# Second input tile of the first quarter loaded in two halves and normalised in two pieces, with the written orders of that quarter replaced

## The chip, the cores and the metric

The kernel runs on one core of one Trainium2 chip. The metric is the device time of one execution in microseconds (us). The kernel before takes 618.46 us, the median of 3 runs that lie between 618.18 and 618.94 us.

## The reference

The input x has 2048 tokens of 640 numbers, all in float32. It is layernormed, goes through an attention and through a feed-forward block, and the product of the two is added to x:

```
xn  = layernorm(x)
qkv = xn @ wqkv                      # 32 heads of 20
for each token s: keys and values of the 8 tokens s, s-2, ..., s-14 (those below 0 masked)
o   = softmax(q . k * 20**-0.5) . v  # over the 8
s   = o @ wo
g   = silu(silu(xn @ w1) @ w2)       # w1 640 x 1536, w2 1536 x 640
out = x + s * g
```

## The kernel before, in words

The tokens are cut into four groups: two halves of the sequence times even and odd positions, since the attention steps by two. A group is four tiles of 128 tokens, numbered 0 to 3. A group's qkv product is made in four quarters of the heads, and a quarter in five chunks of 128 input features. Of each product in float32 three cheaper ones are made: an operand is split into a high part (a copy rounded to the format fp32r) and a low part (what is left), and high times high, low times high and high times low are summed in PSUM. So a weight chunk c of the first quarter goes through three steps: it is loaded by SyncE's DMA queue in two pieces (the q columns, L420, and the k and v columns, L421), its high part is made by ScalarE (`wh` c, L463), and its low part by GpSimd or VectorE (`wl` c, L466; `ON_DVE` lists those that VectorE makes).

The change lies in the first quarter of the first group (`first_quarter`), where nothing has been loaded yet. Tile t is loaded (`xin` t). VectorE takes its statistics over two halves of the row (`s` t `a` and `b`, L694) and joins them (`g` t, L696), ScalarE takes the root (`q` t, L506), VectorE the reciprocal (`r` t, L508) and then normalises the tile (`a` t j, L700). TensorE transposes the five chunks of the tile (`T` t, L729) into PSUM; ScalarE makes the high part of the transposed tile (`h` t j, L740) and VectorE the low part (`l` t j, L744). Tile 0 is treated apart: its transposed tile is also copied whole to SBUF (`f0` j, L707) and multiplied with the raw weights of chunks 0 to 2 in full float32 (`0f0` to `0f2`, two passes each, L756), since the split weights are not ready so early; its high and low parts for chunks 3 and 4 come from that copy (`h02` and `l02`, L714 and L716). All other products of the quarter are of L764. There are 51 of them. A product is written as tile, kind and chunk: `1h0` is tile 1's high part times the high part of weight chunk 0, `1x0` its low part times the high part, `1w0` its high part times the low part.

What sets the order: every operation is recorded with its engine, duration, reads and writes in `Weave`, a small planner. In the first quarter the order is written out by hand: `FIRST` is TensorE's, `ORDER` that of ScalarE, VectorE and GpSimd. The loads on SyncE's queue go by priority numbers: weight chunk k has 1 + k, and `X_AT` gives those of tiles 1 to 3. `EARLY` holds the landing times that the planner assumes for the first transfers. The planner runs when the program is built; on the chip each engine takes its instructions strictly in the order that came out, and waits on semaphores where an operand is not there. Eight semaphores serve SyncE's transfers in turn, so a transfer is issued only when the one eight places ahead has landed. After the first quarter the products of the second quarter follow (L824 to L826).

Of the kernel before, what the change touches and what calls it, by code (L numbers as in the profile page):

```python
# [14 lines left out]
P = 128  # L15
# [3 lines left out]
DC, FC = D // P, F // P  # L19
# [21 lines left out]
NB = P // B  # L41
SHIFT = 16
RUN = D
X_AT = 1.5, 3.5, 5.5
LOW_AT = 3
ON_DVE = (3, 6, 7, 8)
FIRST = """T00 T01 0f0 T02 0f1 T1 0f2 1w1 1h2 1h0 1h1 1x0 1x2 1h3 0h4 1w0 1w2 1x1 1x3 0x3 1h4 0h3 0w4
           0w3 1x4 T2 0x4 1w4 1w3 2w1 2h234 2h1 2w4 2x3 2x2 2x1 2x4 T3 2w23 2h0 2w0 3h2 3w0 3w1 3w4 3x4
           3x1 3x0 3h0 3h4 3h3 3w2 3x3 2x0 3x2 3h1 3w3"""
ORDER = {"ACT": """q0 f00 wh0 f01 q1 wh1 f02 h02 wh2 h10 h11 h12 wh3 wh4 q2 h20 q3 h21 h30 h31 wh5 h00""",  # L50
         "DVE": """wl1 s0a s0b g0 r0 wl2 a00 a01 a02 s1a s1b g1 r1 a10 s2a l10 s2b l11 l02 g2 l12 s3a
                   r2 wl3 a20 s3b g3 l20 l21 r3 a30 l30 l31 l00""",
         "POOL": """wl0 wl4"""}


# [16 lines left out]
class Weave:  # L72
# [8 lines left out]
    LANES = 8  # L81
    RATE = 310e3
    LAND = 1.9
    EARLY = 2.4, 2.9, 4.8, 5.6, 6.95, 8.15, 8.9, 9.9
    TABLE = 1.28
    PATIENCE = 1.8
    SOFT = 2.5
# [65 lines left out]
    def chain(self):  # L153

        for e, names in ORDER.items():
            row = [self.named[n] for n in names.split() if n in self.named and self.named[n].eng == e]
# [84 lines left out]
def local_attention_silu_ffn(ctx: ExitStack, tc: tile.TileContext, x, wqkv, wo, w1, w2, out):  # L241
    nc = tc.nc
# [8 lines left out]
    xg = x.rearrange("b (g p j) d -> (b g) p j d", p=P, j=J)  # L251
# [4 lines left out]
    def rows(view, g):  # L256
        h, par = groups[g]
        return view[h, :, par::2, :]
# [32 lines left out]
    XIN = sb.tile([P, T, D], F32, name="xin")  # L291
# [17 lines left out]
    def bank():  # L309
        i = take("acc", 6)  # L310
        return ACC[i], ("acc", i)
# [22 lines left out]
    def dma(fn, reads, writes, nbytes, prio, dur=0.45, late=0.0):  # L334
        add("SP", dur, fn, reads, writes, prio, nbytes=nbytes, late=late)
# [102 lines left out]
    def w_load():  # L438
# [24 lines left out]
        act(n, lambda: nc.scalar.activation(hi, raw, AF.Copy), kr, [kh], 1000 + due, name=f"wh{k}")  # L463
        pool_does = k < LO and k not in ON_DVE
        eng, cost, by = ("POOL", po(n), nc.gpsimd) if pool_does else ("DVE", dv(n), nc.vector)
# [25 lines left out]
    def load_x(g, t, n=1, prio=None):  # L491
        dma(lambda: nc.sync.dma_start(XIN[:, t:t + n], rows(xg, g)[:, t:t + n]), [],
            [("xin", u) for u in range(t, t + n)], n * P * D * 4, clock[0] if prio is None else prio,
            late=LATE if g else 0.0)
# [179 lines left out]
    def first_quarter(i):  # L674
# [8 lines left out]
        PARTS = ((0, 1), (1, 3), (3, DC)), ((0, 1), (1, 3), (3, DC)), ((0, 3), (3, DC)), ((0, 3), (3, DC))  # L683
        XF = O[:, 0, :]
        steps = FIRST.split()
        total = [sum(len(s) - 2 for s in steps if s[0] == str(t) and s[1] in "hxwf") for t in range(T)]

        def begin(t):

            st, ks = ST[t % 2], ("st", t % 2)  # L690
            for k in range(2):
                cs = slice(k * 320, (k + 1) * 320)
                kx = ("xin", t) if t or k else ("xin", t, "a")
                dve(320, lambda k=k, cs=cs: nc.vector.bn_stats(out=st[:, k, :], in_=XIN[:, t, cs]), [kx], [ks + (k,)], 1,  # L694
                    name=f"s{t}" + "ab"[k])
            dve(60, lambda: nc.vector.bn_aggr(out=MV[:, t, :], in_=st), [ks + (0,), ks + (1,)], [("mv", t)], 1, name=f"g{t}")  # L696
            ln_rstd(t, t + 1, 1, name=str(t))
            for j, (a, b) in enumerate(PARTS[0] if not t else ((0, DC),)):
                cs = slice(a * P, b * P)
                dve((b - a) * 80, lambda cs=cs: nc.vector.tensor_scalar(  # L700
                    out=XIN[:, t, cs], in0=XIN[:, t, cs], scalar1=MV[:, t, 0:1], scalar2=SD[:, 1, t:t + 1],
                    op0=OP.subtract, op1=OP.mult), [("rs", t), ("mv", t), ("xin", t)],
                    [("xn", t, k) for k in ((j,) if not t else range(len(PARTS[t])))], 1, lock=True, name=f"a{t}{j}")

        def full(j, a, b, tp, kp):

# [59 lines left out]
                more = 0.0  # L766

        given = {}
        for k in range(2):
            cs = slice(k * 320, (k + 1) * 320)  # L770
            dma(lambda cs=cs: nc.sync.dma_start(XIN[:, 0, cs], rows(xg, 0)[:, 0, cs]), [],
                [("xin", 0) if k else ("xin", 0, "a")], P * 320 * 4, -2)
        for k, p in enumerate(X_AT):
            load_x(0, k + 1, prio=p)
        for k in range(RING):
            w_load()
        whole = [early_raw[c] for c in range(DC)]
# [4 lines left out]
        for t in range(T):  # L782
            b, kp = bank()
            ps[t] = b, kp
        turned = [0]
        for step in steps:
# [7 lines left out]
            t, k, cs = int(step[0]), "hxwf".index(step[1]), step[2:]  # L794
# [110 lines left out]
    def wo_last(g, i):  # L905
# [23 lines left out]

        ORDER = steps(range(3)) + steps(range(3, DC))  # L930

        def whole(t, cols, a=0, b=15):
            for n in range(a, b):
                x, c, k = ORDER[n]
                tm_mm(banks, t, x[i][:, c, tsl(t)], ws[c][k], n == 0, n == 14, cols)
# [16 lines left out]
        def rest():  # L952
            for n, (x, c, k) in enumerate(ORDER):
                nc.tensor.matmul(lastb[:, :CB], x[i][:, c, tsl(t)], ws[c][k][:, CA:], start=n == 0, stop=n == 14)  # L954
# [115 lines left out]
```

## Time and profile before

| | |
|---|---|
| median of 3 runs | 618.46 us (618.18 to 618.94) |
| the profiled execution | 618.66 us |
| its span from first to last instruction | 616.9 us |
| TensorE busy in the span | 611.0 us (99%) |
| VectorE, ScalarE, GpSimd busy | 563.5, 310.4, 110.3 us |
| share of TensorE in the chain that ended last | 98% |

Times in the views are microseconds from the span's start. The profiled execution took 1.8 us more than its span, for what lies around it. The start of the first quarter is the stretch up to about 23.4 us, when the first product of the second quarter begins.

### The profile page before, as it was taken

The page shows a single profiled execution, that of the slowest core. Times are in us where ns is not written, and L with a number is a line of the kernel's source. Part 1 is how long each engine was busy: PE and PEld are TensorE (multiplying, and loading weights), DVE is VectorE, ACT ScalarE, POOL GpSimd, SP SyncE. Part 2 cuts the span into 40 slices and gives each one's busy share as a digit, 9 for nine tenths or more (in the row PEclk, how much of TensorE's full clock was granted, in tenths as well). Part 3 has the DMA queues.
Part 4 walks back from the last instruction along what each step waited for, and adds up shares of the span by engine and source line. Part 5 has one row for each costly group of instructions (what it writes and reads, how often), then busy time and mean ns, then how long its engine had stood idle before and what let it go on. Part 6 is the DMA issues. An engine that isn't in the chain of part 4 may idle for free.

```text
span 616.9 us, 9054 instructions
## 1 busy us (share of the span) xinstructions
PE 611.0 (99%) x3347; PEld 551.1 (89%) x3347; DVE 563.5 (91%) x584; ACT 310.4 (50%) x656; POOL 110.3 (18%) x167
## 2 busy tenths in 40 slices
PE   8999999999999999999999999999999999999997
PEld 6889999998889999999888999999888999999997
DVE  6578999999989998999999999999979999999964
ACT  5535658937376313851945512582496316152650
POOL 5500000011101133111212233111121213311100
PEclk9999999999999999999999999999999999999999
DMA  8999999867999998764799999955569999866642
GB/s 251 337 281 350 345 371 413 322 222 218 309 295 347 334 358 263 232 198 138 205 240 253 335 333 309 277 179 163 168 198 285 240 320 304 283 213 198 208 149 86
DMA packets 61513, 162.45 MB, mean 263 GB/s; under 512 B 6957, under 2 KB 25229, under 8 KB 61469
## 3 DMA queue, kind: packets, MB, share of 16 engines
q0 software_dynamic: 20016, 82.58, 44.4%
q1 hardware_dynamic: 41453, 79.29, 40.3%
q8 instruction: 26, 0.43, 0.3%
q14 instruction: 18, 0.15, 0.1%
HBM read 109.55 MB, written 34.16 MB: 233 GB/s over the span
## 4 chain that ended last, share of the span: by engine, by line
PE 98%; DMA 1%; DVE 0%; SPq 0%; issue 0%; ACT 0%
PE acc L853 22%; PE acc L856 15%; PE acc L824 10%; PE acc L825 10%; PE acc L826 10%; PE rot L973 9%; PE rot L974 9%; PE rot L972 9%; PE acc L764 2%; DMA xin<-in_A_x_dram 1%; PE rot L856 1%; PE rot L853 0%; PE acc L954 0%; PE rot L729 0%; DVE st L694 0%; PE acc L756 0%
## 5 line engine op out<-in xcount | busy, mean ns | idle before, releaser
L824 PE MATMUL acc<-w,thl 128*128 128x512 f32 (+1 forms) x300 | 112.5, 375 | 0.0
L826 PE MATMUL acc<-w,thl 128*128 128x512 f32 (+1 forms) x300 | 112.4, 375 | 0.0
L825 PE MATMUL acc<-w,thl 128*128 128x512 f32 (+1 forms) x300 | 112.4, 375 | 0.0
L853 PE MATMUL acc<-w,sh 128*128 128x384 f32 x384 | 111.5, 333 | 0.0
L856 PE MATMUL acc<-w,sh 128*128 128x256 f32 x384 | 107.1, 279 | 0.0
L978 ACT ACTIVATE sh<-rot 128x512 fp32r<-128x512 f32 x48 | 28.7, 598 | 146.1 <-PE rot L974 146.0
L974 PE MATMUL rot<-thl,w 128*128 128x512 f32 x240 | 93.6, 390 | 0.0
L973 PE MATMUL rot<-thl,w 128*128 128x512 f32 x240 | 93.6, 390 | 0.0
L972 PE MATMUL rot<-thl,w 128*128 128x512 f32 x240 | 93.5, 389 | 0.0
L662 DVE TENSOR_TENSOR pr<-e,kv 128x2560 f32<-128x2560 f32 x32 | 90.4, 2823 | 0.8
L627 DVE TENSOR_REDUCE l<-pr 128x128 f32<-128x2560 f32 x32 | 90.0, 2813 | 0.6
L624 DVE TENSOR_TENSOR pr<-q,kv 128x2560 f32<-128x2560 f32 x32 | 90.1, 2816 | 0.2
L667 DVE TENSOR_TENSOR pr<-pr 128x1280 f32<-128x1280 f32 x64 | 74.0, 1155 | 1.5
L856 PEld LDWEIGHTS acc<-w,sh 128*128 128x128 f32 x384 | 72.2, 188 | 0.9
L853 PEld LDWEIGHTS acc<-w,sh 128*128 128x128 f32 x384 | 72.1, 188 | 0.9
L451 POOL DMA_DIRECT2D w<-half_w x72 | 38.6, 536 | 190.0 <-PE rot L974 60.8
L451 POOL DMA_DIRECT2D w<-half_q x52 | 27.7, 533 | 242.1 <-PE rot L974 116.8
L824 PEld LDWEIGHTS acc<-w,thl 128*128 128x128 f32 x300 | 56.3, 188 | 8.9 <-ACT gate L1027 0.2
L826 PEld LDWEIGHTS acc<-w,thl 128*128 128x128 f32 x300 | 56.3, 188 | 8.6
L825 PEld LDWEIGHTS acc<-w,thl 128*128 128x128 f32 x300 | 56.3, 188 | 8.6
L853 PE MATMUL acc<-w,thl 128*128 128x384 f32 x225 | 63.1, 333 | 0.0
L540 ACT ACTIVATE xin<-sf 32x256 f32<-32x256 f32 (+1 forms) x144 | 54.6, 379 | 8.2 <-DVE sf L567 6.6
(100 smaller groups left out, 1040.0 us busy)
## 6 DMA issues: line engine op xcount, KB each, us to landing
w<-half_w POOLq DMA_DIRECT2D x72, 640.0 KB, 5.9
w<-half_q POOLq DMA_DIRECT2D x39, 512.0 KB, 4.6
half_w<-w SPq DMA_DIRECT2D x24, 640.0 KB
w<-half_wo POOLq DMA_DIRECT2D x15, 640.0 KB, 5.6
kv<-kv SPq DMA_DIRECT2D x15, 560.0 KB
half_q<-w SPq DMA_DIRECT2D x15, 512.0 KB
kv<-kv SPq DMA_DIRECT2D x15, 420.0 KB
w<-half_q POOLq DMA_DIRECT2D x13, 384.0 KB, 4.9
```

Source lines behind the costliest of these rows:

```text
L624: dve(2560, lambda t=t: nc.vector.tensor_tensor(out=PR, in0=win(qq[:, t:t + 2, :], W, 0), in1=win(kv[:, 0, t:t + 2, :], W, CQ), op=OP.mult ...
L627: dve(2560, lambda t=t: nc.vector.tensor_reduce(out=l[:, t:t + 2].rearrange("p t w h -> p (t w h)"), in_=PR.rearrange("p t w (h d) -> p (t ...
L662: dve(2560, lambda t=t, v=v: nc.vector.tensor_tensor(out=PR.rearrange("p t w (h d) -> p t (w h) d", d=DH), in0=e[:, t:t + 2].rearrange("p ...
L667: dve(2 * k * CQ, lambda k=k: nc.vector.tensor_tensor(out=PR[:, :, 0:k, :], in0=PR[:, :, 0:k, :], in1=PR[:, :, k:2 * k, :], op=OP.add), [] ...
L824: nc.tensor.matmul(o, hi, wh, start=c == 0, stop=False)
L825: nc.tensor.matmul(o, lo, wh, start=False, stop=False)
L826: nc.tensor.matmul(o, hi, wl, start=False, stop=c == DC - 1)
L853: nc.tensor.matmul(a[t][0][:, :CA], st, w[:, :CA], start=first, stop=last)
L856: nc.tensor.matmul(b[t // 2][0][:, h * CB:(h + 1) * CB], st, w[:, CA:], start=first and h == 0, stop=last, skip_group_check=True)
L972: nc.tensor.matmul(h, wh[:, cs], TH[i][:, c, :], start=c == 0, stop=False)
L973: nc.tensor.matmul(h, wh[:, cs], TL[i][:, c, :], start=False, stop=False)
L974: nc.tensor.matmul(h, wl[:, cs], TH[i][:, c, :], start=False, stop=c == DC - 1)
```

## The change

Tile 1 is loaded as tile 0 already was: two transfers of 320 columns each in place of one of 640. Its first statistics wait for the first half alone. It is normalised in two pieces, of chunks 0 to 2 and of chunks 3 and 4, and each piece has its own successors among the transposes. The priorities of tiles 2 and 3 on the load queue go from 3.5 and 5.5 to 5.5 and 7.5. The low parts of weight chunks 1 and 5 go from GpSimd to VectorE and that of chunk 7 from VectorE to GpSimd. `FIRST`, `ORDER` and `EARLY` have new contents.

```diff
-X_AT = 1.5, 3.5, 5.5
+X_AT = 1.5, 5.5, 7.5
-ON_DVE = (3, 6, 7, 8)
-FIRST = """T00 T01 0f0 T02 0f1 T1 0f2 1w1 1h2 1h0 1h1 1x0 1x2 1h3 0h4 1w0 1w2 1x1 1x3 0x3 1h4 0h3 0w4
+ON_DVE = (1, 3, 5, 6, 8)
+FIRST = """T00 T01 T02 0f0 0f1 T101 T12 0f2 1h0 1w1 1x2 1h2 1w2 1h1 1x0 0h3 1h3 1x4 1h4 1w4 0w4 0h4 0x4
...
-    EARLY = 2.4, 2.9, 4.8, 5.6, 6.95, 8.15, 8.9, 9.9
+    EARLY = 2.4, 2.9, 5.3, 5.7, 6.1, 6.95, 8.3, 9.15, 9.95
...
-                kx = ("xin", t) if t or k else ("xin", t, "a")
+                kx = ("xin", t) if t > 1 or k else ("xin", t, "a")
...
-            for j, (a, b) in enumerate(PARTS[0] if not t else ((0, DC),)):
+            for j, (a, b) in enumerate((PARTS[0], ((0, 3), (3, DC)))[t] if t < 2 else ((0, DC),)):
...
-                    [("xn", t, k) for k in ((j,) if not t else range(len(PARTS[t])))], 1, lock=True, name=f"a{t}{j}")
+                    [("xn", t, k) for k in ((j,) if not t else ((0, 1), (2,))[j] if t == 1 else range(len(PARTS[t])))], 1, lock=True, name=f"a{t}{j}")
...
-        for k in range(2):
-            cs = slice(k * 320, (k + 1) * 320)
-            dma(lambda cs=cs: nc.sync.dma_start(XIN[:, 0, cs], rows(xg, 0)[:, 0, cs]), [],
-                [("xin", 0) if k else ("xin", 0, "a")], P * 320 * 4, -2)
-        for k, p in enumerate(X_AT):
-            load_x(0, k + 1, prio=p)
+        for t in range(2):
+            for k in range(2):
+                cs = slice(k * 320, (k + 1) * 320)
+                dma(lambda t=t, cs=cs: nc.sync.dma_start(XIN[:, t, cs], rows(xg, 0)[:, t, cs]), [],
+                    [("xin", t) if k else ("xin", t, "a")], P * 320 * 4, X_AT[0] if t else -2)
+        for k, p in enumerate(X_AT[1:]):
+            load_x(0, k + 2, prio=p)
```

On SyncE's queue, after tile 0 and weight chunk 0, this stands before (xin is an input tile, pr holds weight chunks 0 to 4, xr and raw the chunks 5 and 6):

```order
L492 DMA xin<-in_A_x_dram 128x640
L420 DMA pr<-in_A_wqkv_dram 128x192
L421 DMA pr<-in_A_wqkv_dram 128x2x160
L420 DMA pr<-in_A_wqkv_dram 128x192
L421 DMA pr<-in_A_wqkv_dram 128x2x160
L492 DMA xin<-in_A_x_dram 128x640
L420 DMA pr<-in_A_wqkv_dram 128x192
L421 DMA pr<-in_A_wqkv_dram 128x2x160
L420 DMA pr<-in_A_wqkv_dram 128x192
L421 DMA pr<-in_A_wqkv_dram 128x2x160
L492 DMA xin<-in_A_x_dram 128x640
```

and this after the change:

```order
L772 DMA xin<-in_A_x_dram 128x320 x2
L420 DMA pr<-in_A_wqkv_dram 128x192
L421 DMA pr<-in_A_wqkv_dram 128x2x160
L420 DMA pr<-in_A_wqkv_dram 128x192
L421 DMA pr<-in_A_wqkv_dram 128x2x160
L420 DMA pr<-in_A_wqkv_dram 128x192
L421 DMA pr<-in_A_wqkv_dram 128x2x160
L420 DMA pr<-in_A_wqkv_dram 128x192
L421 DMA pr<-in_A_wqkv_dram 128x2x160
L492 DMA xin<-in_A_x_dram 128x640
L420 DMA xr<-in_A_wqkv_dram 128x192
L421 DMA xr<-in_A_wqkv_dram 128x2x160
```

Tile 1 is two transfers in the same place. Tile 2 has moved from between chunks 2 and 3 to behind chunk 4, and tile 3 from in front of chunk 5 to behind chunk 6.

On VectorE, from the statistics of tile 1 on, this stands before (st1 and st0 are statistics, thl0 the transposed tiles' high and low parts, w3_77 the split weight chunk 3):

```order
L694 BN_STATS st1_81<-xin_100 128x6 x2
L696 BN_AGGR mv_69<-st1_81 128x2
L508 RECIPROCAL sd_86<-sd_86 128x1
L700 TENSOR_SCALAR xin_100<-xin_100,mv_69,sd_86 128x640
L694 BN_STATS st0_72<-xin_100 128x6
L744 TENSOR_TENSOR thl0_67<-rot0_111,thl0_67 128x128
L694 BN_STATS st0_72<-xin_100 128x6
L744 TENSOR_TENSOR thl0_67<-rot1_112,thl0_67 128x2x128
L716 TENSOR_TENSOR thl0_67<-o_94,thl0_67 128x2x128
L696 BN_AGGR mv_69<-st0_72 128x2
```

and this after the change:

```order
L694 BN_STATS st1_81<-xin_100 128x6 x2
L696 BN_AGGR mv_69<-st1_81 128x2
L508 RECIPROCAL sd_86<-sd_86 128x1
L700 TENSOR_SCALAR xin_100<-xin_100,mv_69,sd_86 128x384
L700 TENSOR_SCALAR xin_100<-xin_100,mv_69,sd_86 128x256
L466 TENSOR_TENSOR w1_75<-pr_95,w1_75 128x512
L744 TENSOR_TENSOR thl0_67<-rot0_111,thl0_67 128x128
L744 TENSOR_TENSOR thl0_67<-rot1_112,thl0_67 128x2x128
L744 TENSOR_TENSOR thl0_67<-acc5_110,thl0_67 128x2x128
L694 BN_STATS st0_72<-xin_100 128x6 x2
L696 BN_AGGR mv_69<-st0_72 128x2
L716 TENSOR_TENSOR thl0_67<-o_94,thl0_67 128x2x128
```

The normalisation of tile 1 is in two pieces, the low part of weight chunk 1 stands right behind it, and the statistics of tile 2 have moved behind the low parts of tile 1.

On TensorE, from the first transposes on, this stands before (rot and acc4, acc5 hold transposes, acc0 and acc1 the products of tiles 0 and 1):

```order
L729 MATMUL rot1_112<-ident_65,xin_100 128x128 x2
L756 MATMUL acc0_105<-pr_95,o_94 128x512
L729 MATMUL acc4_109<-ident_65,xin_100 128x128 x2
L756 MATMUL acc0_105<-pr_95,o_94 128x512
L729 MATMUL rot0_111<-ident_65,xin_100 128x128
L729 MATMUL rot1_112<-ident_65,xin_100 128x128 x2
L729 MATMUL acc5_110<-ident_65,xin_100 128x128 x2
L756 MATMUL acc0_105<-pr_95,o_94 128x512
L764 MATMUL acc1_106<-w1_75,thl0_67 128x512
L764 MATMUL acc1_106<-w2_76,thl0_67 128x512
L764 MATMUL acc1_106<-w0_74,thl0_67 128x512
```

and this after the change:

```order
L729 MATMUL rot1_112<-ident_65,xin_100 128x128 x2
L729 MATMUL acc4_109<-ident_65,xin_100 128x128 x2
L756 MATMUL acc0_105<-pr_95,o_94 128x512 x2
L729 MATMUL rot0_111<-ident_65,xin_100 128x128
L729 MATMUL rot1_112<-ident_65,xin_100 128x128 x2
L729 MATMUL acc5_110<-ident_65,xin_100 128x128 x2
L756 MATMUL acc0_105<-pr_95,o_94 128x512
L764 MATMUL acc1_106<-w0_74,thl0_67 128x512
L764 MATMUL acc1_106<-w1_75,thl0_67 128x512
L764 MATMUL acc1_106<-w2_76,thl0_67 128x512 x3
L764 MATMUL acc1_106<-w1_75,thl0_67 128x512
```

The last transposes of tile 0 have moved ahead of the first full product, and the first split product is now of chunk 0 instead of chunk 1. Sixteen split products stand ahead of tile 2's transposes where eighteen stood, and eleven between those and tile 3's where thirteen stood. ScalarE's order changes in one place that matters here: the copy of tile 0's last chunks comes ahead of chunk 1's high part, and the high part of chunk 4 ahead of chunk 3's.

## Rows read from the trace of the kernel before

**Rows 1.** The page: TensorE's busy time, and the chain's shares by engine.
```profile
PE 611.0 (99%) x3347; PEld 551.1 (89%) x3347; DVE 563.5 (91%) x584; ACT 310.4 (50%) x656; POOL 110.3 (18%) x167
...
PE 98%; DMA 1%; DVE 0%; SPq 0%; issue 0%; ACT 0%
```

**Rows 2.** Stretches: length, busy per engine (instructions), granted clock, DMA share, GB/s.
```profile
5.30:9.11 3.81, 3.15 (x10) 1.21 (x10) 2.46 (x7) 2.35 (x7) 1.57 (x2) 1.00 1.01 324
9.11:23.43 14.32, 14.32 (x68) 11.47 (x69) 9.63 (x21) 7.78 (x22) 6.84 (x6) 1.00 0.96 315
23.43:613.40 589.97, 589.88 (x3253) 534.98 (x3251) 548.41 (x541) 298.52 (x626) 99.28 (x154) 1.00 0.85 264
```

**Rows 3.** Chain of waits, first 24 us: start, length, what held the end.
```profile
2.63 4.10 DMA xin<-in_A_x_dram
6.75 0.90 DVE st L694 x2
...
8.44 0.62 DVE xin L700
9.11 0.55 PE rot L729 x3
```

**Rows 4.** Timeline of TensorE: start, length, instruction, count, idle before and its releaser.
```profile
7.59 1.10 PE L756 MATMUL acc<-pr,o 128*128 128x512 f32 x2 [0.23 <-DMA pr<-in_A_wqkv_dram]
9.11 0.55 PE L729 MATMUL rot<-ident,xin 128*128 128x128 f32 x3 [0.42 <-DVE xin L700]
...
9.71 1.02 PE L756 MATMUL acc<-pr,o 128*128 128x512 f32 x2
10.54 4.36 PE L764 MATMUL acc<-w,thl 128*128 128x512 f32 x18
14.75 0.71 PE L729 MATMUL rot<-ident,xin 128*128 128x128 f32 x5
15.21 3.27 PE L764 MATMUL acc<-w,thl 128*128 128x512 f32 x13
...
18.78 4.81 PE L764 MATMUL acc<-w,thl 128*128 128x512 f32 x20
23.43 0.39 PE L824 MATMUL acc<-w,thl 128*128 128x512 f32 x1
```

**Rows 5.** Timeline of SyncE's queue: issues, as in rows 4.
```profile
0.76 0.87 SPq L771 DMA_DIRECT2D xin<-in_A_x_dram  x2
...
8.95 0.38 SPq L421 DMA_DIRECT2D xr<-in_A_wqkv_dram  x1
```

**Rows 6.** Waits of SyncE's queue, first 24 us: us in total, times, longest.
```profile
SPq L421 <- DMA pr<-in_A_wqkv_dram: 0.4, 1, 0.4
```

**Rows 7.** Normalisations of the first quarter: ns shortest/median/longest, and their shapes.
```profile
L700 DVE TENSOR_SCALAR xin<-xin,mv,sd x6: 346/506/614, 4.9 to 16.8; 128x640 f32<-128x640 f32 x3, 128x256 f32<-128x256 f32 x2, 128x128 f32<-128x128 f32 x1
```

**Rows 8.** Timeline of VectorE, 9 to 16 us.
```profile
9.78 0.49 DVE L694 BATCH_NORM_STATS2 st<-xin 128x6 f32<-128x320 f32 x1 [0.73 <-DMA xin<-in_A_x_dram]
...
12.63 1.29 DVE L466 TENSOR_TENSOR w<-pr,w 128x512 fp32r<-128x512 f32 x1
...
15.01 0.67 DVE L466 TENSOR_TENSOR w<-raw,w 128x512 fp32r<-128x512 f32 x1
```

**Rows 9.** Timeline of ScalarE, 8 to 14 us.
```profile
8.63 0.36 ACT L707 ACTIVATE o<-acc 128x256 f32<-128x256 f32 x1
...
9.35 0.62 ACT L463 ACTIVATE w<-pr 128x512 fp32r<-128x512 f32 x1
9.87 0.53 ACT L740 ACTIVATE thl<-rot 128x128 fp32r<-128x128 f32 x2
...
11.37 0.63 ACT L463 ACTIVATE w<-pr 128x512 fp32r<-128x512 f32 x1 [0.15 <-DMA pr<-in_A_wqkv_dram]
...
13.73 0.64 ACT L463 ACTIVATE w<-raw 128x512 fp32r<-128x512 f32 x1 [1.55 <-DMA raw<-in_A_wqkv_dram]
```

**Rows 10.** Timeline of GpSimd, 12 to 14 us.
```profile
12.07 1.29 POOL L466 TENSOR_TENSOR w<-pr,w 128x512 fp32r<-128x512 f32 x1 [0.64 <-ACT w L463]
```

More of the change, by code (lines that the diff above doesn't have):

```diff
@@ L43 @@
 RUN = D
-X_AT = 1.5, 3.5, 5.5
+X_AT = 1.5, 5.5, 7.5
 LOW_AT = 3
-ON_DVE = (3, 6, 7, 8)
-FIRST = """T00 T01 0f0 T02 0f1 T1 0f2 1w1 1h2 1h0 1h1 1x0 1x2 1h3 0h4 1w0 1w2 1x1 1x3 0x3 1h4 0h3 0w4
[L48 to L52, printed above, removed]
+ON_DVE = (1, 3, 5, 6, 8)
+FIRST = """T00 T01 T02 0f0 0f1 T101 T12 0f2 1h0 1w1 1x2 1h2 1w2 1h1 1x0 0h3 1h3 1x4 1h4 1w4 0w4 0h4 0x4
+           1x1 T2 0x3 1x3 1w0 2h1 2w2 0w3 1w3 2h3 2h2 2w1 2w4 T3 2w0 2x3 2h0 2x1 3h2 3h3 3w0 2x0 3h4
+           2h4 3x3 2x4 3w1 3w4 3x0 3h0 3w3 2x2 3w2 3x4 3x2 2w3 3h1 3x1"""
+ORDER = {"ACT": """q0 f00 wh0 f01 q1 f02 wh1 wh2 h10 h11 h02 h12 wh4 wh3 q2 h20 h21 q3 h30 h31 h00 wh5""",
+         "DVE": """s0a wl2 s0b g0 r0 a00 a01 a02 s1a s1b g1 r1 a10 a11 wl1 l10 l11 l12 s2b s2a g2 l02
+                   r2 a20 s3b s3a wl3 g3 l20 r3 a30 l21 l31 l30 l00""",
          "POOL": """wl0 wl4"""}
```

## The prediction

> **What bounds the kernel now.** I read the page first. TensorE is busy in 99% of the span, and 98% of the chain that ended last is TensorE [rows 1]; nothing is to be had but time in which it stands still. The busy time by stretches says where that is: from 9.11 to 23.43 us it is busy in 14.32 of 14.32 us, from there to 613.40 us in 589.88 of 589.97 us, but from 5.30 to 9.11 us in only 3.15 of 3.81 us [rows 2]. At 23.43 us the second quarter begins [rows 4]. The work behind it is left as it is and nothing there waits, so the question is when that first product of the second quarter starts, and the shift is carried whole to the end. The chain of waits names the hole: tile 1's load, issued at 2.63 us, holds the end until 6.73 us, then its two statistics, its normalisation, and TensorE takes its transposes at 9.11 us [rows 3]. TensorE's timeline shows two pauses there: 0.23 us before the second full product, which waits for weight chunk 1, and 0.42 us before tile 1's transposes [rows 4]. From then on it runs without a pause. So there is a ceiling: the third full product, at 9.71 us, needs chunk 2, and that landed at about 8.94 us, as the issue at 8.95 us was released by a landing after a wait of 0.4 us [rows 5, 6]. No more than 9.71 - 9.0 = 0.7 us can come from the hole.
>
> **The change part by part.** The load queue first. An issue of a half takes 0.44 us (0.87 us for two) [rows 5], so one transfer more delays each later issue by that. I cost it at nothing: the DMA engines are busy all through the stretch from 5.30 us (share 1.01) [rows 2], so a later issue finds a queue still full. If that cover is gone, chunk 1 lands 0.44 us later, and the lead worked out below falls by about 0.35 us. For the landings I take those of before, since the bytes stand in the same order up to chunk 2: chunk 1 at 7.5 us (TensorE's wait ended at 7.59), the last byte of tile 1 at 6.73, chunk 2 at 8.94. Tile 2 landed at about 9.75 us [rows 8], so a tile takes 9.75 - 8.94 = 0.81 us of the queue. Half of it is 0.4, which puts tile 1's first half at about 6.3 us. With tile 2 moved behind chunks 3 and 4, chunk 4 lands at 11.3 - 0.81 = 10.5 (before, ScalarE's wait for it ended at 11.37) and tile 2 where chunk 4 stood, at 11.3. Tile 3 takes the place of chunk 6, which landed at 13.7 [rows 9].
>
> The statistics: two take 0.90 us [rows 3] and one 0.49 [rows 8]. The first now runs while the second half lands, and the chain loses 0.41 us. The second starts at 6.75 and ends at 7.24; join, root and reciprocal take 8.44 - 7.65 = 0.79 [rows 3], so the normalisation starts at 8.03. Its pieces are 384 and 256 wide; between the 346 ns of the 128 wide one and the 614 ns of the 640 wide one [rows 7] they take 0.48 and 0.41 us. They end at 8.51 and, overlapping a little, 8.92; TensorE followed 0.05 us behind before. The second full product starts at 7.59 as before and leaves TensorE free at about 8.5. The transposes come at 8.57 (three) and 8.97 (two, to 9.19), the third full product at 9.19, and the first split product at 9.19 + 0.83 = 10.02 (before, 9.71 to 10.54) [rows 4]. The lead is 0.52 us. Moving tile 0's last transposes ahead of the first full product costs 0.22 us, inside the pause before 7.59.
>
> From there each engine's new order has to keep up, and here part of the lead goes back.
> - ScalarE: after the root at 7.8 come tile 0's copy (0.36) and chunk 1's high part (0.6), then chunk 2's, which must wait for 8.94. It starts 0.35 us sooner than before (9.35), and the high parts of tile 1 follow 0.52 us behind, two in 0.53 us, to 10.05 [rows 9].
> - VectorE: chunk 1's low part (0.67, the row at 15.01) from 8.92 to 9.6, then tile 1's low parts, the second ending at 10.55 (its high part's end plus about 0.5). The third split product needs it: 10.6 instead of 10.48, so 0.12 us is lost.
> - The high parts of chunks 4 and 3: ScalarE is through with the tiles' at 10.65, so they end at 11.2 and 11.75. The product that wants chunk 3's is in turn at 11.75 and starts at 11.8. With 9 products of 0.23 us TensorE reaches tile 2's transposes at 13.87.
> - Tile 2: tile 1 took 9.11 - 6.73 = 2.38 us from landing to transposes. 11.3 + 2.38 = 13.7, and a low part of tile 0 that now stands in that chain adds up to 0.3. I take 13.95. Before, those transposes came at 14.75 with 18 split products done; now 16 will be, so the like moment is 14.75 - 2 x 0.23 = 14.29, and the lead is 0.34.
> - Tile 3: its statistics start when tile 2 is normalised, at 13.9, and take 0.9; chunk 3's low part adds 0.67, join and root 0.79, a low part in between 0.2, the normalisation 0.61: transposes at 17.1. TensorE's own stream is there at 13.95 + 0.46 + 11 x 0.23 = 16.94.
> - The end: 17.1 + 0.46 + 24 x 0.2325 (20 products took 23.43 - 18.78) = 23.14 [rows 4]. With tile 3's small wait hidden it is 22.98.
>
> So the second quarter begins 0.29 to 0.45 us sooner; I take 0.35. The low parts of chunks 5 and 7 change engines at 0.67 and 1.29 us; chunk 5's is not wanted before 23.1 and chunk 7's two chunks later, so I count nothing.
>
> The profiled execution took 618.66 us; less 0.35 that is 618.31. It lay 0.20 above the median of the runs, 618.46, against which the new kernel is seen: 618.1 us.
>
> A row speaks against moving low parts to VectorE: the one at 12.63 us took 1.29 us [rows 8] while GpSimd made its own from 12.07 to 13.36 [rows 10], and the one at 15.01, with GpSimd idle, 0.67. The Trainium skill, page "SBUF — State Buffer", section "SBUF: two separate sides", has a rule for it: the port pair that VectorE and GpSimd share "is an exclusive lock, not a bandwidth split"; whoever comes second waits for the whole instruction of the first. The trace agrees: 12.63 + 1.29 = 13.92, which is 0.56 us after GpSimd's end. By it the sum stays where it is as long as VectorE's low part of chunk 1 comes ahead of GpSimd's of chunk 2; where it comes behind, see the last rival.
>
> **The rivals.**
> - The hole closes fully. For it: the waits that I find behind 10.02 us are 0.05 to 0.16 us each, and landings that are 0.1 or 0.2 us sooner remove them. Then the lead is what chunk 2's landing leaves, 0.5 to 0.7: 617.9 us.
> - The halves do nothing. Tile 1 is spread over the engines that move it, and the last share of either half could land at 6.7. Then only the split normalisation is left, 0.61 - 0.48 = 0.13 us: 618.3. Against it: the two halves of tile 0 are issued 0.44 us apart, and the queue is in order.
> - Tile 2 takes the place of tile 1: slower. It now lands behind five weight chunks, and its transposes come 2.65 us behind its landing. Below a landing at 11.3 it hides; from 14.29 - 2.65 = 11.65 on the kernel is slower than before, 1 us for 1 us, and tile 3 behind it shifts alike. For it: the later issues wait for landings, and every transfer in front is issued 0.44 us later. A landing at 12.1 gives 618.46 + 0.45 = 618.9. Against it: the queue moved its bytes at a share of 0.96 in all of 9.11 to 23.43 us [rows 2], so a gap that long would be new.
> - The shared port: if VectorE's low part of chunk 1 starts after GpSimd's of chunk 2 (9.7 us, against 8.92 by the sum), it ends at about 9.7 + 1.29 + 0.56 = 11.55, the second split product waits from 10.25 to 11.6, and all low parts queue behind it: 1.35 - 0.35, so 619.4 us. The margin is 0.8 us, and what delays tile 1 delays chunk 2 as well.
>
> **How the numbers follow.** My forecast (a lead of 0.2 to 0.5) gets 0.48, the full hole 0.17, the halves without effect 0.18, tile 2 late 0.13, the port 0.04. The runs before spread over 0.76 us, so I add some 0.2 on both sides: 617.5 to 618.9 holds eight in ten; the forecast's own range is 617.9 to 618.3. A measurement of this kernel can tell about 0.2% from no change, and that is 1.24 us: faster means below 617.2, more than the ceiling gives, so it is left 0.05 for what I don't see; slower means above 619.7 and needs two of the bad cases together, 0.05.
>
> **What would show it.** The first statistics of tile 1 should start at about 6.35 and the second at 6.75; the transposes at 8.6; the first split product at 10.0; tile 2's transposes near 13.95, tile 3's near 17.1, and the first product of the second quarter near 23.1. The forecast is wrong if the second full product starts later than 7.7 (the issue was not hidden), if ScalarE's high part of chunk 2 does not start near 9.0, if tile 2 lands after 11.6, or if TensorE pauses anywhere behind 23.1 us.

## The result and the profile after

The changed kernel takes 619.41 us, the median of 20 runs (618.87 to 621.37), beside 618.50 us for the kernel before (20 runs, 618.18 to 619.17). The ratio is 1.0015, 95% interval 1.0008 to 1.0022: 0.9 us longer where 0.35 us less was forecast, and outside the range. That is 0.15%; the interval leaves out 1. The profiled execution is one of the long ones, 620.88 us with a span of 619.1; a second profile of the same kernel, taken later, has 619.17 us and stands beside it below.

The page, as in [rows 1]: TensorE's busy time, and the chain's shares by engine.

```profile
PE 611.8 (99%) x3347; PEld 552.0 (89%) x3347; DVE 561.0 (91%) x586; ACT 310.8 (50%) x656; POOL 108.5 (18%) x166
...
PE 86%; DMA 8%; SPq 3%; DVE 2%; issue 1%; ACT 0%; DVEq 0%; ACTq 0%
```

TensorE has lost 12% of the chain to transfers, to SyncE's queue and to VectorE. The stretches of [rows 2] again, their ends moved to the second quarter's new start and to the last matmul (columns as there):

```profile
5.30:9.11 3.81, 3.60 (x12) 1.90 (x12) 3.10 (x9) 2.62 (x7) 1.26 (x1) 1.00 0.84 240
9.11:23.65 14.54, 14.35 (x70) 11.28 (x69) 9.36 (x24) 8.92 (x23) 3.42 (x3) 1.00 1.00 330
23.65:615.20 591.55, 589.94 (x3253) 535.00 (x3251) 545.53 (x540) 297.50 (x625) 101.20 (x156) 1.00 0.86 263
```

Three things stand there. The hole up to 9.11 us looks nearly closed (3.60 of 3.81 us busy, before 3.15). The DMA engines, which moved 324 GB/s in it, now move 240. And behind 23.65 us there is idle time, 1.6 us, where before there was 0.1. The second profile has the first stretch thus:

```profile
5.30:9.11 3.81, 3.12 (x12) 1.32 (x12) 2.67 (x9) 2.45 (x7) 1.26 (x1) 1.00 0.85 250
```

So the hole isn't closed there: TensorE is busy for 3.12 us, as little as before. In the first profile its early work took longer, for a reason that no row shows: the two passes of the first full product last 1.37 us, in the second profile 1.02. TensorE's timeline of the first profile, as in [rows 4]:

```profile
8.03 1.10 PE L756 MATMUL acc<-pr,o 128*128 128x512 f32 x2 [0.21 <-DMA pr<-in_A_wqkv_dram]
8.97 0.49 PE L729 MATMUL rot<-ident,xin 128*128 128x128 f32 x3
...
9.97 2.18 PE L764 MATMUL acc<-w,thl 128*128 128x512 f32 x7
12.35 2.37 PE L764 MATMUL acc<-w,thl 128*128 128x512 f32 x9 [0.19 <-ACT w L463]
14.55 0.71 PE L729 MATMUL rot<-ident,xin 128*128 128x128 f32 x5
15.01 2.77 PE L764 MATMUL acc<-w,thl 128*128 128x512 f32 x11
17.62 0.71 PE L729 MATMUL rot<-ident,xin 128*128 128x128 f32 x5
18.09 5.72 PE L764 MATMUL acc<-w,thl 128*128 128x512 f32 x24
23.65 0.39 PE L825 MATMUL acc<-w,thl 128*128 128x512 f32 x1
```

The first split product comes at 9.97, as forecast (10.02). In the second profile the second full product starts at 7.85, after one long wait for weight chunk 1:

```profile
7.85 1.10 PE L756 MATMUL acc<-pr,o 128*128 128x512 f32 x2 [0.69 <-DMA pr<-in_A_wqkv_dram]
```

Back in the first profile, the eighth split product waits until 12.35, for ScalarE. ScalarE's timeline, as in [rows 9], says for what:

```profile
10.08 0.38 ACT L740 ACTIVATE thl<-acc 128x256 fp32r<-128x256 f32 x1
11.14 1.15 ACT L463 ACTIVATE w<-pr 128x512 fp32r<-128x512 f32 x2 [0.68 <-DMA pr<-in_A_wqkv_dram]
```

It stands idle until 11.14 for weight chunk 4, and only then makes two high parts, chunk 4's and chunk 3's. The chain of waits, as in [rows 3], leads from there back to the queue:

```profile
6.53 0.47 SPq L420
6.99 0.04 issue
7.04 4.02 DMA pr<-in_A_wqkv_dram
...
11.68 0.62 ACT w L463
12.30 0.04 issue
12.35 2.37 PE acc L764 x9
```

Ahead of the 7.04 us stand 13 issues, one per 0.48 us, with no gap over 0.06 us. In the second profile the chain goes another way, through the landing of tile 2:

```profile
7.51 4.72 DMA xin<-in_A_x_dram
...
12.26 0.90 DVE st L694 x2
...
13.95 0.62 DVE xin L700
...
14.62 0.77 PE rot L729 x5
```

When transfers landed (us, the last byte, read from the semaphore events of the traces):

```
                          chunk 1  chunk 2  chunk 3  chunk 4  tile 2  tile 3
before                      7.45     8.94    10.50    11.28     9.76   12.13
forecast                    7.5      8.94             10.5     11.3    13.7
after                       7.90     8.67     9.88    11.06    11.96   14.37
after, second profile       7.72     8.47     9.33    10.87    12.23   14.62
```

Behind the first quarter there is one wait of TensorE (engine and line, what it waited for, us in total, times, longest):

```profile
PE acc L854 <- DVE sl L981: 1.5, 1, 1.5
```

It begins at about 87.7 us and ends at 89.28, for a low part of the feed-forward block, and the second profile doesn't have it. Last, the end. Both kernels finish with VectorE's last addition; then come the last store and SyncE's closing waits. The span and the last row of the chain, before:

```profile
core 0 of [0], span 616.9 us
...
613.81 0.42 DVE xin L921
```

and after:

```profile
core 0 of [0], span 619.1 us
...
615.62 0.42 DVE xin L922
```

Before, 616.9 - 613.81 = 3.1 us from there to the end; after, 3.5. All profiles of this study in one table, with the medians (us; to the start of the last matmul, and from there to the end of the span):

```
                        2nd quarter  to last  to the  profiled  median (range), n          ratio to before
                        begins       matmul   end     run
before                    23.43      589.60    3.83    618.66   618.50 (618.18-619.17) 20
after                     23.65      591.20    4.26    620.88   619.41 (618.87-621.37) 20  1.0015 [1.0008, 1.0022]
after_again               23.77      589.39    4.25    619.17   619.21 (618.85-620.84) 11  1.0011 [1.0002, 1.0019]
behind_after              23.18      589.38    3.83    618.18   618.26 (617.90-618.50) 11  0.9995 [0.9986, 1.0004]
behind_after2             22.95      589.56    3.83    618.13   618.25 (618.08-619.69) 11  0.9994 [0.9984, 1.0004]
behind_before             24.60      589.39    4.24    620.02   619.73 (619.44-620.17) 11  1.0019 [1.0010, 1.0027]
behind_before_dve         24.83      589.62    4.25    620.47   619.91 (619.65-620.47) 10  1.0022 [1.0013, 1.0031]
behind_before_sp          23.09      589.39    4.24    618.52   619.01 (618.52-620.13) 11  1.0008 [1.0000, 1.0017]
behind_before2            23.40      589.45    4.26    618.90   619.25 (618.61-621.00) 11  1.0011 [1.0002, 1.0019]
x1_on_act                 23.11      591.67    4.25    620.83   619.09 (618.68-620.92) 11  1.0014 [1.0005, 1.0023]
chunk3_first              23.42      590.86    4.26    620.31   619.26 (618.89-621.89) 11  1.0010 [0.9999, 1.0022]
halves_alone              23.50      589.75    4.25    619.29   619.63 (619.29-619.84) 11  1.0016 [1.0007, 1.0025]
x2_late_alone             24.36      589.61    3.83    619.60   619.65 (619.35-620.08) 11  1.0017 [1.0008, 1.0026]
x2_back                   24.05      589.38    4.25    619.48   619.72 (619.48-621.11)  9  1.0020 [1.0011, 1.0030]
after_merged_end          23.66      590.06    3.82    619.31   618.83 (618.49-620.47) 11  1.0004 [0.9995, 1.0012]
before_split_end          23.36      589.60    4.25    619.00   618.97 (618.80-619.86) 11  1.0009 [1.0000, 1.0018]
x1_on_act_merged_end      23.04      589.39    3.83    618.03   618.50 (618.03-620.05) 11  1.0001 [0.9992, 1.0010]
x1_whole_on_act           25.00      589.38    3.85    620.02   619.95 (618.64-620.23) 11  1.0016 [1.0006, 1.0026]
```

The usual execution of the changed kernel is that of after_again: 0.34 us later at the second quarter, 0.21 less behind it, 0.42 more at the end, together 0.55; its profiled time is 0.51 above that of before, and its median 0.56 above that of the before runs beside it (618.65). The first profile has 1.8 us more behind 23.65 us. The first row has a weakness that bears on all that follows: behind_after, behind_after2 and before_split_end have the first quarter of before unaltered, and their second quarters begin at 23.18, 22.95 and 23.36. The 23.43 of before is the latest of the four.

### The profile page after: what moved, and what is told of

The parts are those of the page before. It is cut to its first block, busy times and chain, and to the rows that moved or that the text cites. A ratio compares the mean times of both kernels' runs of the same rounds, so it can differ in the third digit from the quotient of the medians.

```text
span 619.1 us, 9062 instructions
## 1 busy us (share of the span) xinstructions
PE 611.8 (99%) x3347; PEld 552.0 (89%) x3347; DVE 561.0 (91%) x586; ACT 310.8 (50%) x656; POOL 108.5 (18%) x166
## 4 chain that ended last, share of the span: by engine, by line
PE 86%; DMA 8%; SPq 3%; DVE 2%; issue 1%; ACT 0%; DVEq 0%; ACTq 0%
PE acc L854 21%; PE acc L857 14%; PE acc L827 8%; PE acc L826 8%; PE acc L825 8%; PE rot L974 8%; PE rot L975 8%; PE rot L973 8%; DMA raw<-in_B_w_dram 3%; DMA half_w<-w 2%; DMA kv<-kv 2%; SPq L592 1%; DMA xin<-in_A_x_dram 1%; PE acc L764 1%; DVE pr L624 1%; DMA pr<-in_A_wqkv_dram 1%
## 5 line engine op out<-in xcount | busy, mean ns | idle before, releaser
L854 PE MATMUL acc<-w,sl 128*128 128x384 f32 x192 | 57.4, 333 | 1.5 <-DVE sl L981 1.5
```

The costliest lines, as they stand in the source:

```text
L854: nc.tensor.matmul(a[t][0][:, :CA], st, w[:, :CA], start=first, stop=last)
```

## The experiments

**Is it the order behind the first quarter?** The planner gave the work behind it another order too. In these kernels that order is forced to be the other kernel's, by a table in the planner's choice (cut; the table LATER, which lists the operations by number, is left out):

```diff
+                if e in LATER:
+                    c = [o for o in c if o.seq not in forced or o.seq == LATER[e][at_later[e]]]
...
```

behind_after is the kernel before with the later orders of the changed one; behind_before, behind_before_sp and behind_before_dve are the changed kernel with those of before, on SyncE, VectorE and ScalarE together, on SyncE alone, and on VectorE and ScalarE. TensorE's order behind the first quarter is the same in every kernel of this study.

> The kernel before, but behind the first quarter SyncE, VectorE and ScalarE take their work in the order of the changed kernel. Theory A (the order behind makes the wait): 619.1 to 619.3 us, with TensorE waiting for VectorE's low parts at about 88 us, while the second quarter begins at 23.4 us as before. Rival B (the first quarter makes it): 618.5 us and no wait.

> The changed kernel, but behind the first quarter SyncE, VectorE and ScalarE take their work in the order of the kernel before; the first quarter is left as changed. Theory A: the new kernel loses about 0.2 us in the first quarter (its second quarter begins at 23.65 us, against 23.43) and the rest of its 0.9 us to a wait of TensorE at 88 us that the new order behind the first quarter makes; so here 618.7 us, with no wait of TensorE behind 24 us and its second quarter at 23.65 us again. Rival B: the order behind is innocent, and the wait comes from what the first quarter leaves behind (later transfers); then 619.4 us as in the changed kernel, with the wait at 88 us still there.

> The changed kernel with SyncE's queue alone in the order of before behind the first quarter (VectorE's and ScalarE's orders stay those of the changed kernel, save for two or three places). Theory A1, the queue of transfers makes the wait at 88 us: 618.7 us, no wait. Theory A2, VectorE's and ScalarE's order makes it: 619.4 us with the wait. Rival B, the first quarter makes it: 619.4 us too.

> The changed kernel with VectorE and ScalarE in the order of before behind the first quarter, and SyncE's queue as in the changed kernel save for one place (the next group's tiles are loaded behind a weight chunk as in the kernel before or not is left to the planner). Theory A1, the queue of transfers makes the wait: 619.2 to 619.4 us, the wait is still there. Theory A2, VectorE's and ScalarE's order: 618.7 us and no wait.

behind_after is not slower, its median is the lowest of the study, though not beyond its interval: the new order is innocent of the 0.9 us. In both profiles of this kernel 0.2 us that before loses at 445 us, in two steps of 0.11 us, are not lost. But behind_before, behind_before_sp and behind_before2, which have orders of before, don't lose them either; so what saves them isn't shown to be the order on these engines. behind_before and behind_before_dve lost 1 us in the first quarter by an accident of the table: a GpSimd memset came forward there. VectorE's timeline in behind_before (start, length) shows what it met:

```profile
13.68 1.73 DVE L775 TENSOR_SCALAR xin<-xin,mv,sd 128x640 f32<-128x640 f32 x1
```

and GpSimd's:

```profile
13.10 1.96 POOL L906 MEMSET kv<- 2x2240 f32 x1
```

The normalisation takes 1.73 us instead of 0.61 [rows 7], and ends 0.35 us after the memset. These two say nothing on the order. behind_before_sp showed something else, the first quarter almost as it was forecast. Its timeline of TensorE:

```profile
9.89 4.24 PE L782 MATMUL acc<-w,thl 128*128 128x512 f32 x16
13.97 0.71 PE L747 MATMUL rot<-ident,xin 128*128 128x128 f32 x5
14.43 2.78 PE L782 MATMUL acc<-w,thl 128*128 128x512 f32 x11
17.05 0.71 PE L747 MATMUL rot<-ident,xin 128*128 128x128 f32 x5
17.51 5.75 PE L782 MATMUL acc<-w,thl 128*128 128x512 f32 x24
23.09 0.39 PE L843 MATMUL acc<-w,thl 128*128 128x512 f32 x1
```

In that execution chunk 4 landed at 10.47 and tile 2 at 11.50. So the forecast's chain holds where its landings do. Its issues on SyncE's queue up to there start at the same times as in the changed kernel, to 0.02 us; what let chunk 4 land 0.6 us sooner in this execution isn't shown. And 23.09 is a lead of 0.34 us on 23.43 alone; behind_after2, with the first quarter of before, began at 22.95.

**Again, and without the memset.** after_again is the changed kernel unaltered; behind_before2 has the orders of before on SyncE, VectorE and ScalarE with GpSimd's own.

> The changed kernel once more, for a second profile and for times beside the three that follow. Every theory: 619.2 to 619.5 us. Where does it lie? Theory F (the first quarter as loaded): chunk 4's landing (11.06 us in the first profile, 10.5 by the forecast) sets how long TensorE waits at 11.8 us; a profile with a landing near 10.5 begins the second quarter at 23.1 us, one near 11.1 at 23.6. Theory L (late wait): whatever the first quarter does, a wait of TensorE for VectorE's low parts at about 88 us adds 0 to 1.6 us, and makes most of the 0.9 us.

> The changed kernel with SyncE, VectorE and ScalarE in the order of before behind the first quarter, and GpSimd in the changed kernel's own order throughout (in the first trial of this a memset of GpSimd had come forward into the first quarter, where it took 1.96 us and VectorE's normalisation beside it 1.73 us in place of 0.61, so that trial says nothing). Theory L with the order behind as its cause: 618.7 us and no wait at 88 us. Theory F: 619.2 to 619.4 us, as changed.

They agree to 0.04 us. The theory of the later order has fallen; the late wait comes in some executions and not in others.

**The first quarter's landings.** In x1_on_act tile 1's halves are issued by ScalarE's queue; in chunk3_first ScalarE makes chunk 3's high part before chunk 4's, with the products to match. Both, and those of the next group, also have a table that keeps the order behind the first quarter (the diffs are cut).

```diff
-                dma(lambda t=t, cs=cs: nc.sync.dma_start(XIN[:, t, cs], rows(xg, 0)[:, t, cs]), [],
+                dma(lambda t=t, cs=cs: (nc.scalar if t else nc.sync).dma_start(XIN[:, t, cs], rows(xg, 0)[:, t, cs]), [],
```

```diff
-h12 wh4 wh3 q2
+h12 wh3 wh4 q2
```

> The changed kernel with all orders kept, but the two halves of tile 1 are issued by ScalarE's queue, which is idle from 2.25 to 4.3 us, in place of SyncE's. So SyncE issues every weight chunk 0.95 us sooner. Theory F, with the issue rate of SyncE's queue as the limit of the landings (0.95 us for a chunk of 262 KB): chunk 1 lands near 7.2 in place of 7.9 us, chunk 4 near 10.3 in place of 11.06, TensorE's waits at 10 to 12.4 us go, the second quarter begins at 22.9 to 23.1 us, and the time falls by 0.5 to 0.7 us to some 618.7 (with the late wait as it is). Rival: the DMA engines are the limit and the landings stay; 619.2 to 619.4 us.

> The changed kernel with ScalarE making chunk 3's high part ahead of chunk 4's, and TensorE taking products that are ready (1x1, 1x3, 1w0, 0h4) ahead of the low part of chunk 4; everything else in the changed kernel's order. Theory F with ScalarE's wait for chunk 4 as the cause: the waits of TensorE at 11.8 and 12.35 us (0.47 us together) go, tile 2's transposes come at about 14.35 us (tile 2's landing then decides) and the second quarter begins at about 23.4 us: 0.2 to 0.3 us less than the changed kernel, about 619.1 us. Theory L: no more than 0.1 us less.

With two issues fewer in front of them chunk 1 lands at 6.85 and chunk 4 at 10.31, although tile 0's second half lands later (4.23 for 3.50); the second quarter begins at 23.11, the forecast's time. With chunk 3 first it begins at 23.42. That is inside what the changed first quarter gave with its own order (23.09 to 23.77 in five profiles), and tile 2 landed sooner here (11.77), so what ScalarE's order costs isn't shown. The times hardly fell, though. Both profiles have the late wait, and both have the longer end.

**One part of the change at a time.** halves_alone: only tile 1's halves and its normalisation in two pieces, all orders of before. x2_late_alone: only tiles 2 and 3 moved, with their statistics behind the low parts, and two operations of ScalarE swapped. x2_back: the changed kernel with tiles 2 and 3 where they were.

```diff
-X_AT = 1.5, 3.5, 5.5
+X_AT = 1.5, 5.5, 7.5
-r1 a10 s2a l10 s2b l11 l02 g2 l12 s3a r2 wl3 a20 s3b g3
+r1 a10 l10 l11 l02 l12 s2a s2b g2 r2 wl3 a20 s3a s3b g3
```

(This is x2_late_alone, without ScalarE's line and the table; x2_back undoes the first two lines in the changed kernel.)

> The kernel before with one part of the change: tile 1 in two halves, normalised in two pieces (its transposes in two steps); tiles 2 and 3, the low parts and all orders stay as before. Theory Q (SyncE issues one transfer per 0.47 us, and what the change lost is the fat transfer of tile 2 that filled the queue between chunks 2 and 3): with it in its old place the extra issue costs little, chunk 4 lands at 11.2 to 11.5, the hole shrinks by 0.2 to 0.4 us, second quarter at 23.0 to 23.3, 618.1 to 618.4. Theory H (the extra issue itself delays every landing behind it by 0.4): chunk 4 lands at 11.7, second quarter at 23.7, 618.8 to 619.0.

> The kernel before with the other part: tile 1 in one transfer as before, tile 2 loaded behind weight chunk 4 and tile 3 behind chunk 6, with the statistics of tiles 2 and 3 moved behind the low parts that would wait for them; all else as before. Theory Q: chunks 3 and 4 follow chunk 2 in eight thin issues, so chunk 4 lands at 10.7 to 11.0 instead of 10.5, tile 2 at 11.8 to 12.0, its transposes at 14.5 to 14.8, second quarter at 23.4 to 23.7: 618.5 to 618.8. Theory H (the delay is the extra issue of tile 1's half, which is not there): chunk 4 at 10.5, tile 2 at 11.3, second quarter at 23.43 as before: 618.5. If this kernel is over 619.0, moving tile 2 alone makes the change slower.

> The changed kernel with tile 2 loaded between weight chunks 2 and 3 again and tile 3 in front of chunk 5; orders of the engines as in the changed kernel. Theory Q: the queue is kept full by tile 2, chunk 4 lands at about 11.2 and tile 2 at 9.8; TensorE's order, made for chunk 4 at 10.5, waits about 0.3 to 0.8 us for the high parts of chunks 4 and 3, but tile 2 no longer waits; second quarter at 23.3 to 23.6, 618.6 to 619.0. Theory H: every landing is 0.4 later than before, chunk 4 at 11.7, second quarter at 24.0 or later, 619.3 or more.

By the landings: chunk 4 at 11.45, 10.26 and 11.48 us, tile 2 at 9.91, 11.37 and 9.93. Moving the tiles alone gives the landings that the forecast counted on (10.5 and 11.3), so the order of the bytes was right. What the extra issue costs is seen only over several profiles, for the landings of one order differ from execution to execution. With tile 2 between the chunks, chunk 4 landed at 10.82 to 11.28 in the four profiles without the extra issue (mean 11.12) and at 11.45 and 11.48 with it. With tile 2 behind chunk 4, it landed at 10.26, 10.31 and 10.49 where SyncE doesn't make that issue (x2_late_alone, x1_on_act, x1_on_act_merged_end; mean 10.35), and at 10.47 to 11.32 in the eight where it does (mean 10.92). So the extra issue delays chunk 4 by some 0.35 us in the one place and 0.6 in the other; theory H, which said 0.4 in both, is borne out as to what delays. Theory Q had x2_late_alone's landings at least 0.4 us too late; whether thin transfers behind the issue make it worse, the spread doesn't let one tell. x2_back waits 0.91 us for chunk 4's high part, since its orders want that early. x2_late_alone is slow by a fault of mine in VectorE's order: the row of TensorE

```profile
15.16 0.74 PE L848 MATMUL acc<-w,thl 128*128 128x512 f32 x2 [1.13 <-DMA gate<-in_A_wqkv_dram]
```

names a transfer that had long landed. What came last was chunk 3's low part on VectorE, which ran at 14.43 behind a low part that had waited 1.08 us for its high part. So this kernel's time says nothing on moving tile 2. halves_alone gave the hint that mattered: its second quarter begins 0.07 us late, and it is 1 us slower than the before runs beside it, as much as the whole change. It has the longer end, x2_late_alone has not. The end is not all of it: the profile is its fastest run, 0.63 us above that of before, and the 0.34 us from there to its median are in no profile.

**The end.** Is it the number of transfers? after_merged_end joins the last two loads of x into one, before_split_end cuts one of them in two, 15 us before the end. x1_on_act_merged_end adds the first to the edit of x1_on_act, without a table. (The diff is that of after_merged_end.)

```diff
-        for t in range(T):
+        for t in range(2):
             dma(lambda t=t: nc.sync.dma_start(xr[t], rows(xg, g)[:, t, :]), [], [kx[t]], P * D * 4, clock[0] - 20)
+        dma(lambda: nc.sync.dma_start(XIN[:, 2:4], rows(xg, g)[:, 2:4]), [], [kx[2], kx[3]], 2 * P * D * 4, clock[0] - 20)
```

> The changed kernel with one transfer less at the end: the last loads of x for tiles 2 and 3 (at about 597 us, wanted at 607) are one transfer of two tiles. Theory C (the number of transfers decides on which of the eight semaphores the last store lands, and the end looks at them in a fixed order, 0.06 us each): from the last matmul's start to the end of the span 3.83 us as before the change, so 619.3 - 0.42 = 618.8 to 619.0. Theory D (the end is longer for another reason that comes with the halves): 4.25 us, 619.2 to 619.4.

> The kernel before with one transfer more at the end: the last load of x for tile 3 (at about 597 us, wanted at 611) in two halves; nothing else changes. Theory C: from the last matmul's start to the end 4.25 us instead of 3.83, 618.6 + 0.42 = 619.0. Theory D: 3.83 us, 618.6.

> The changed kernel with tile 1's halves issued by ScalarE's queue and the last loads of x merged. If the three parts add up: second quarter at 23.1 to 23.2 (0.3 sooner than before), 0.2 less behind it by the later order, the end as before, so 618.0 to 618.3 in most executions; some executions with the late wait at about 87.5 us, 1.5 us longer, stay. If the end keeps its 0.42 us: 618.5 to 618.8.

The first two are shown to 0.01 us: 3.82 and 4.25. The waits of SyncE's queue at the end (waiting line, releaser, us, times, longest), in after_merged_end:

```profile
SPq L1067 <- DMA out_dram<-xin: 0.8, 1, 0.8
```

and in before_split_end:

```profile
SPq L1067 <- DMA out_dram<-xin: 1.2, 1, 1.2
```

At the end SyncE waits for all semaphores in a fixed order, 0.06 us for each. The transfers take eight of them in turn, and before the change the last store has the one that is looked at last: the other waits pass while it is in flight. One transfer more, and it has the first of the eight: SyncE waits for it 1.2 us, and the seven that follow cost 7 x 0.06 = 0.42 us when nothing else is left to do. x1_on_act_merged_end has both parts mended; its profile is its fastest run, 618.03, and its median of 618.50 isn't to be told from before.

**Fewer issues than before?** x1_whole_on_act is behind_after with the whole of tile 1 issued by ScalarE's queue; behind_after2 ran beside it.

> The same kernel as behind_after (the kernel before with the changed kernel's order behind the first quarter), for comparison on the same chip: 618.2 to 618.4, second quarter at 23.2 to 23.4, 589.4 us from there to the last matmul, 3.83 from there to the end.

> behind_after with the whole of tile 1 issued by ScalarE's queue, which is idle then; nothing else changes, the number of transfers neither. If landings go by the issues ahead of them on SyncE's queue: weight chunks 1 to 4 and tiles 2 and 3 land about 0.45 us sooner than in behind_after, tile 1 too, second quarter at 22.7 to 23.0, 617.8 to 618.0. If the DMA engines set the landings (the bytes are the same): chunks as before, second quarter at 23.1 to 23.3, 618.2. If tile 1's early transfer delays tile 0 and weight chunk 0 by as much as it takes away: later than 23.4, 618.5 or more.

It was the third case. Chunk 1 lands at 6.50 for 7.08, but tile 1, issued at 0.92 us, shares the engines with tile 0, whose second half lands at 4.91 for 3.53, so the work on it starts 1.4 us later and the second quarter at 25.00 for 22.95. Chunk 4 lands no sooner (11.18 for 10.82, and 11.11 in behind_after), so in this profile one issue less on SyncE's queue brought nothing.

## Why the prediction was wrong

- **The hole: right as to VectorE, wrong as to TensorE.** Tile 1's halves landed at 5.72 and 6.26 (forecast 6.3 and 6.73; in the second profile 5.73 and 6.94). The transposes came at 8.97 and 8.79 instead of 8.57, held by the second full product and not by VectorE. But that product waited for chunk 1 and started at 8.03 and 7.85, beyond the 7.7 that the prediction named as the sign of a visible issue. The third full product started at 9.51 and 9.39 where 9.19 was forecast and 9.71 stood before, so of the lead of 0.52 us there were 0.2 to 0.3. That the first split product still starts at 9.97 is luck: the 0.83 us that the sum put in front of it was 0.46, and the second split product started at 10.61 (forecast 10.25, before 10.85).
- **"I cost it at nothing": wrong, and this is the step that failed.** The extra issue was to be hidden because "a later issue finds a queue still full". The DMA engines were full before at a share of 1.01 [rows 2]; in the changed kernel the share of that stretch is 0.84. Four profiles of the first quarter of before have 0.94 to 1.01, and each part of the change alone is below: it is 0.87 in halves_alone, where tile 2 has its old place, and 0.89 in x2_late_alone, where there is no extra issue. I took a number of the old order for the new one. Chunk 1 landed 0.3 to 0.45 us later, as the text's own other branch said; what it missed is chunk 4, at 10.9 to 11.1 instead of 10.5, and tile 2 behind it. (Chunk 2 came sooner than forecast, at 8.67 and 8.47.) The third split product, at 10.83 instead of 10.6, has lost 0.2 us by the first; the eighth waits for a high part and stands at 12.35 instead of 11.8. These 0.55 us are the difference between the forecast 23.1 and 23.65. The Trainium skill, page "Perfetto Trace Analysis", section "What "DMA-bound" means", lists the queue that issues beside the engines that move: a sequencer track that is solid with DMA slices is a bound of its own. The trace agrees as far as the track goes: SyncE's has no gap over 0.06 us from 0.76 to 8.45 us. It doesn't show that the issues alone set the landings, for behind_before_sp has the same track and landed chunk 4 at 10.47.
- **Tile 2 in place of tile 1: it happened, at about the price given.** The rival's turning point was a landing at 11.65. It landed at 11.96 and 12.23. 11.96 + 2.65 = 14.61 against transposes at 14.55; in the second profile they came at 14.62, 2.39 behind the landing, and it is this landing that the chain there goes through. So the late chunk 4 and the late tile 2 hide behind each other. By an estimate from the traces either alone would have cost some 0.4 us: in the first profile tile 2 was normalised at 14.29, in the second TensorE was through with its products at 14.37, and 13.95 was forecast.
- **The shared port: it did not happen.** VectorE's low part of chunk 1 started at 8.64 and took 0.69 us.
- **The lead was counted from one execution.** 23.43 was the latest of four profiles of that first quarter; their mean is 23.23. The changed one, as it was planned, has 23.09 to 23.77 in five profiles (after, after_again, after_merged_end, behind_before_sp, behind_before2), with a mean of 23.51. So it is some 0.3 us later and not 0.35 sooner, with an overlap.
- **"Carried whole to the end": wrong.** The end is 0.42 us longer, a term that the sum put at nothing. The text ahead of the prediction names the eight semaphores and the diff shows one transfer more; I read neither for the end.
- **"Nothing there waits": wrong in some executions.** The wait at 87.7 us is in the profiles at 620.3 us and more of after, x1_on_act and chunk3_first, and in part (0.4 us) in after_merged_end. By it I read the runs over 620 us, 2 of 20 in after, 4 of 11 in x1_on_act; this is a guess, as few of them have a profile, and the kernel before has such runs too, 4 of 158. In after a feed-forward weight issued at 52.40 us lands at 61.02, and the next issue waits for that semaphore until 61.09; in after_again it is issued at 51.38, lands at 58.91, and the next issue comes at 58.98. In after ScalarE then waits 2.9 us for a transfer of these weights. What makes those transfers late in one execution and not in the next is open.

Of the 0.9 us then 0.42 is the end (shown, in both directions). Some 0.3 is the first quarter instead of a gain of 0.35 (a difference of means, not beyond the spread of single executions). 0.2 comes off behind it, by what isn't shown. Together that is 0.5, which is what the second profile and the 0.56 us of its runs say; the rest of the 0.9 is the spread between executions and the late wait, which no run took apart.

## What to carry to other kernels

Count issues as well as bytes: a DMA share of 1.0 belongs to the order in which it was measured, and both a transfer cut in two and a large one moved away lowered it here. Take the start of a stretch from several executions before forecasting a few tenths of a microsecond. Where a shift is to be carried to the end, look at what the end waits for, and in which order; one transfer more or less can move it. The kernel with the lowest median here left the first quarter alone.

## What the hardware showed that was not expected

- The closing waits: 0.42 us by the place of the last store among eight semaphores, in both directions.
- The GpSimd memset of 13.10 us touches 2 partitions, and VectorE's 128x640 normalisation beside it takes 1.73 us instead of 0.61. It ends 0.35 us behind the memset, and so it does in behind_before_dve. That fits the lock between the two that the forecast cited (the Trainium skill, "SBUF — State Buffer", "SBUF: two separate sides"), here for a memset.
- The same transfer, in the same place, lands up to 0.85 us apart in two executions: chunk 4 at 10.47 to 11.32 us in eight profiles with the extra issue and tile 2 behind chunk 4. In the four with the first quarter of before it landed at 10.82 to 11.28.
